# A linear-attention kernel with a token-wise maxout stage: attention stages dealt over slots, features dealt 3p+s, weights loaded second

## Chip, core and metric

The kernel runs on one core of a Trainium2 chip. What counts is the device time of one execution in microseconds. The core's engines run side by side, each through its own list of instructions in order, and wait for each other only where data or buffers ask for it: TensorE (PE, matmuls; PEld is its loading of weights), VectorE (DVE), ScalarE (ACT), GpSimd (POOL) and SyncE (SP, which issues the transfers).

## What is computed

Gated linear attention over 4 x 8 heads with 768 tokens and head size 48, then a maxout stage on the 3072 tokens with the 8 x 48 = 384 features of all heads:

```python
for t in range(S):
    state = alpha[:, :, t, :, None] * state + np.einsum('bhd,bhe->bhde', k[:, :, t], v[:, :, t])
    y[:, :, t] = np.einsum('bhd,bhde->bhe', q[:, :, t], state)
x = y.transpose(0, 2, 1, 3).reshape(B * S, H * D)
h1 = x @ w1
h2 = x @ w2
out = np.maximum(h1, h2) @ w_out
```

All inputs and the output are fp32; w1 and w2 are 384 x 1024, w_out is 1024 x 384.

## The kernel before

The recurrence is cut into chunks of 128 tokens, six for each of four batches, so 24 chunks `n`; a chunk covers all eight heads, taken as four pairs. The stages of a chunk are small functions:

- `load` (L62): four transfers (alpha, q, k, v) of 128 x 8 x 48 floats, issued by SP. Six buffers each.
- `a1` (ACT): `loga`, the logarithm of alpha. `p1` (PE): `cs`, its running sums by a triangular matrix, and four tiny matmuls for the decay of each half. `a2` (ACT): `en`, `ep`, `gg`, exponentials of it.
- `v1`: `qt` (DVE) and `kt` (POOL) are q and k times those; POOL also casts v into `v16`. `vt` (POOL) decays the running state `w` of the chunk before into `T16` and `t32`.
- `p2` (PE): eight transposes into `tp`; `v2` (DVE): `qk`, a copy of it. `p3` (PE): scores `pa`, `pb` and, in a batch's first five chunks, the state's increment `kv`. `v3` (DVE): two masked products `pt` and the new state `w`.
- `p4` (PE): y of the chunk, twelve matmuls of 96 output rows in four column groups, a head pair each (eight in a batch's first chunk). `a3` (ACT): copies it to `xT[0:96]`. So `xT` holds four head pairs of 96 features as four slabs. The maxout stage contracts 384 features as three slabs of 128: every third chunk, three transfers on ACT's queue (L265) move the fourth pair into rows 96 to 127 of the other three.

The maxout stage works on windows of 384 tokens, as max(h1, h2) = relu(h1 - h2) + h2. `fstep` (8 per window): three matmuls into a bank `h`, emptied through a relu into `g16` by DVE (three of eight) or ACT. `tstep` (one per 128 tokens): three matmuls with `m16` = w2 w_out and eight with `g16` and `wo16` into `op`; ACT copies it to `outs`, SP stores it. `prep_cast`, `prep_t` and `prep_m` make `wd16` = w1 - w2, `wo16` and `m16` once.

The order is written out by hand. A slot `n` is: `p2(n)`, `v2(n)`, `a2(n+1)`, gap 0, `a1(n+2)`, `p3(n)`, `v1(n+1)`, `v3(n)`, `vt(n+1)`, gap 1, `p1(n+2)`, `p4(n)`, `a3(n)`, gap 2. The gaps hold steps of the maxout stage by a fixed table: the eight `fstep`s of a window lie in the gaps of the slots after its last chunk, its `tstep`s in gap 2 of three slots after that. The last windows run after the last chunk. SP's list begins with chunks 0 to 2 and then the weights; chunk n+3 is issued in slot n. Matmul results lie in PSUM banks: `psx` (three: `cs`, `tp`, `kv`), `psp` (two: `pa`, `pb`) and `psm` (three: `y`, `h`, `op`).

Of the kernel before, what the change touches and what calls it, by code (L numbers as in the profile page):

```python
# [16 lines left out]
def kernel(  # L17
# [18 lines left out]
    nc = tc.nc  # L36
# [8 lines left out]
    W = 384  # L45
    CPW = W // C
    NW = NT // W
# [9 lines left out]

    nc.scalar.preload_act_table_set("natural_log_exp_and_others")
# [14 lines left out]
    for n in range(3):  # L73
        load(n)
# [49 lines left out]
    def a1(n):  # L124
        if n >= NCG:
            return
        af = loads[n][0]
        nc.scalar.activation(out=logas[n % NB][:, :, 0:D], in_=af, func=ACTF.Ln)  # L128

    def p1(n):  # L130
        if n >= NCG:
            return
        loga = logas[n % NB]
# [8 lines left out]
    def a2(n):  # L142
# [6 lines left out]
        gg = wk.tile([128, NP, 2], FP32, tag="gg", bufs=3)  # L149
# [19 lines left out]
    def vt(n):  # L169
        if n >= NCG:  # L170
            return
        s = st[n]
        if n % NCH:
            g = wk.tile([128, NP], FP32, tag="g")
            nc.gpsimd.tensor_mul(out=g[0:112], in0=st[n - 1]["gg"][0:112, :, 1], in1=s["gg"][0:112, :, 0])
            gb = g[0:112].unsqueeze(2).to_broadcast([112, NP, D])
            w = st[n - 1]["w"]
            T16 = T16s[n % 2]
            nc.gpsimd.tensor_mul(out=T16[0:48, :, 0:D], in0=w[0:48], in1=gb[0:48])  # L179
            nc.gpsimd.tensor_mul(out=T16[64:112, :, D : 2 * D], in0=w[64:112], in1=gb[64:112])  # L180
# [15 lines left out]
    def v2(n):  # L196
        qk = wk.tile([128, 2 * NP, 128], FP16, tag="qk")
# [201 lines left out]
```

## Time and profile before

| | us |
|---|---|
| median of 3 runs | 212.19 (212.09 to 214.8) |
| the profiled execution's own time | 212.77 |
| its span, first to last instruction | 211.0 |

| engine | busy us of the span | instructions |
|---|---|---|
| TensorE, matmul | 154.2 | 1440 |
| VectorE | 92.6 | 153 |
| ScalarE | 76.6 | 188 |
| GpSimd | 89.6 | 168 |

Busy time of TensorE counts each matmul from its start to its modelled end; matmuls overlap, so what they take in a row is read from their starts. The views that follow below are the windows (busy time of PE, PEld, DVE, ACT and POOL, in this order, in a stretch, with the granted clock of TensorE as a share of 2.4 GHz and what DMA moved), the waits (who waited for whom), the chain of waits (the work that ended last, followed back), the timeline and the groups of instructions by line. A chunk's slot is the unit in which to read them. L12 is line 12 of the kernel.

### The profile page before, as it was taken

To read this page: it belongs to the slowest core of one execution; us is meant where nothing else is said; L and a number is where in the kernel's file an instruction comes from. 1 tells how busy PE (TensorE), PEld (TensorE's weight loads), DVE (VectorE), ACT (ScalarE), POOL (GpSimd) and SP (SyncE) were. 2 spreads that over 40 slices of the span, in tenths; PEclk is the share of its full clock that TensorE was granted. 3 is DMA by queue.
4 is the path that set the end of the run, shared out by engine and by line. 5 is a ranking of instruction groups with operands and counts; after the bars stand their busy time and mean duration, and the time that the engine had idled before them with its cause. 6 is when DMAs were issued, how large, how long until landed. Compare 5 with 4: busy or idle time off the path is not lost.

```text
span 211.0 us, 3834 instructions
## 1 busy us (share of the span) xinstructions
PE 154.2 (73%) x1440; PEld 103.8 (49%) x1440; DVE 92.6 (44%) x153; ACT 76.6 (36%) x188; POOL 89.6 (42%) x168
## 2 busy tenths in 40 slices
PE   1182003757997599878888897988598988889993
PEld 1161002546665466455555564556365655555651
DVE  4255000776436557255655457344515755431200
ACT  3421000312553454434545425442424544315411
POOL 7267505654523575355335555342326545300000
PEclk9999999999999979999999999799859999999999
DMA  7999999999999006589777898389549741012122
GB/s 131 190 201 223 233 284 237 166 201 172 202 174 150 15 0 127 116 148 188 150 143 141 161 176 171 70 151 185 118 82 185 148 96 40 7 36 84 48 91 89
DMA packets 106339, 29.16 MB, mean 138 GB/s; under 512 B 100688, under 2 KB 105552, under 8 KB 106320
## 3 DMA queue, kind: packets, MB, share of 16 engines
q1 hardware_dynamic: 105168, 28.32, 70.6%
q10 hardware_dynamic: 1152, 0.59, 1.2%
q8 instruction: 11, 0.18, 0.4%
q14 instruction: 8, 0.07, 0.1%
HBM read 23.59 MB, written 4.72 MB: 134 GB/s over the span
## 4 chain that ended last, share of the span: by engine, by line
PE 37%; DVE 18%; SPq 15%; issue 10%; ACT 8%; ACTq 6%; DMA 4%; DVEq 0%
SPq L67 14%; PE op L313 12%; DVE pt L230 12%; PE y L251 7%; ACTq L265 6%; PE h L300 5%; PE op L311 5%; DVE qt L162 3%; DVE qk L198 3%; ACT xT L261 2%; PE mp L288 2%; DMA af<-in_alpha_dram 2%; PE y L247 2%; DMA xT<-xT 2%; ACT outs L316 2%
## 5 line engine op out<-in xcount | busy, mean ns | idle before, releaser
L163 POOL TENSOR_TENSOR kt<-kf,en 128x384 f16<-128x384 f32 x24 | 23.9, 996 | 56.6 <-ACT en L150 49.1
L300 PE MATMUL h<-xT,wd 128*128 128x384 f16 x192 | 42.0, 334 | 0.3 <-ACT outs L316 0.3
L198 DVE COPY qk<-tp 128x1024 f16<-128x1024 f16 x24 | 16.5, 689 | 56.1 <-PE tp L193 56.1
L313 PE MATMUL op<-wo,g 128*128 128x384 f16 x192 | 37.4, 341 | 0.0
L251 PE MATMUL y<-pt,v 128*96 128x128 f16 x192 | 24.8, 240 | 12.7 <-DVE pt L230 12.3
L261 ACT CAST xT<-y 96x512 f16<-96x512 f32 x24 | 14.0, 582 | 49.9 <-PE y L251 49.9
L135 PE MATMUL cs<-loga,cmat 128*128 128x384 f16 x24 | 8.9, 370 | 30.5 <-ACT loga L128 26.0
L162 DVE TENSOR_TENSOR qt<-qf,ep 128x384 f16<-128x384 f32 x24 | 23.1, 962 | 14.5 <-ACT ep L151 13.8
L303 DVE TENSOR_SCALAR g<-h 128x384 f16<-128x384 f32 x24 | 13.2, 550 | 30.8 <-PE h L300 30.8
L313 PEld LDWEIGHTS <-g 128*128 128x128 f16 x192 | 19.6, 102 | 14.1 <-issue 2.7
L316 ACT COPY outs<-op 128x384 f32<-128x384 f32 x24 | 11.5, 479 | 40.3 <-PE op L313 23.4
L139 PEld LDWEIGHTS <-loga 128*112 128x112 f16 x96 | 10.2, 152 | 31.8 <-issue 29.7
L251 PEld LDWEIGHTS <-v 128*96 128x96 f16 x192 | 20.1, 140 | 8.7 <-issue 8.4
L305 ACT ACTIVATE g<-h 128x384 f16<-128x384 f32 x40 | 19.9, 500 | 8.6 <-PE h L300 6.1
L128 ACT ACTIVATE loga<-af 128x384 f16<-128x384 f32 x24 | 12.9, 537 | 26.9 <-DMA af<-in_alpha_dram 25.0
L300 PEld LDWEIGHTS <-wd 128*128 128x128 f16 x192 | 16.7, 100 | 8.7 <-issue 0.9
L179 POOL TENSOR_TENSOR T<-w,g 48x192 f16<-48x192 f32 x20 | 10.0, 499 | 22.5 <-DVE w L238 16.6
L166 POOL CAST v<-vf 128x192 f16<-128x192 f32 x24 | 18.3, 761 | 0.0
L247 PE MATMUL y<-qk,T 112*96 112x128 f16 x80 | 17.4, 238 | 0.0
L230 DVE TENSOR_TENSOR pt<-pa,u 128x512 f16<-128x512 f32 x24 | 16.3, 680 | 2.2 <-PE pb L207 2.1
L207 PE MATMUL pa<-qk 48*128 48x128 f16 x96 | 10.5, 236 | 8.6 <-DVE qk L198 8.6
L311 PE MATMUL op<-m,xT 128*128 128x384 f16 x72 | 16.6, 342 | 0.0
(51 smaller groups left out, 211.2 us busy)
## 6 DMA issues: line engine op xcount, KB each, us to landing
af<-in_alpha_dram SPq DMA_DIRECT2D x24, 192.0 KB, 3.5
qf<-in_q_dram SPq DMA_DIRECT2D x24, 192.0 KB, 3.9
kf<-in_k_dram SPq DMA_DIRECT2D x24, 192.0 KB, 4.2
vf<-in_v_dram SPq DMA_DIRECT2D x24, 192.0 KB, 4.4
out_dram<-outs SPq DMA_DIRECT2D x24, 192.0 KB, 2.0
wof<-in_moe_w_out_dram SPq DMA_DIRECT2D x1, 1536.0 KB, 19.1
w2f<-in_moe_w_dram SPq DMA_DIRECT2D x1, 1152.0 KB, 9.2
w1f<-in_moe_w_dram SPq DMA_DIRECT2D x1, 1152.0 KB, 14.6
```

What stands on the lines that cost most here:

```text
L67: nc.sync.dma_start(out=t, in_=src[b, :, c * C : (c + 1) * C, :].rearrange("h p d -> p h d"))
L162: nc.vector.tensor_mul(out=qts[n % 2][:, :, 0:D], in0=qf, in1=s["ep"])
L163: nc.gpsimd.tensor_mul(out=kts[n % 2][:, :, 0:D], in0=kf, in1=s["en"])
L166: nc.gpsimd.tensor_copy(out=v16[:, :, 0:D], in_=vfp[:, :, 0, :])
L198: nc.vector.tensor_copy(out=qk, in_=st[n]["tp"])
L230: nc.vector.tensor_mul(out=pt[:, t], in0=s["pp"][t], in1=ub)
L247: nc.tensor.matmul(y[0:96, r, :], lhsT=T16s[n % 2][0:112, r, :], rhs=s["qk"][0:112, r, :], start=True, stop=False)
L251: nc.tensor.matmul(y[0:96, r, :], lhsT=v16[:, r, 48 * t : 48 * t + 96], rhs=s["pt"][:, t, r, :], start=(n % NCH == 0 and t == 0), stop=(t ...
L300: nc.tensor.matmul(h, lhsT=wd16[:, s, f * 128 : (f + 1) * 128], rhs=xT[:, s, w * W : (w + 1) * W], start=(s == 0), stop=(s == 2))
L305: nc.scalar.activation(out=gts[w][:, f, :], in_=h, func=ACTF.Relu)
L311: nc.tensor.matmul(op, lhsT=xT[:, s, t0 : t0 + 128], rhs=m16[:, s, :], start=(s == 0), stop=False)
L313: nc.tensor.matmul(op, lhsT=gts[w][:, f, i * 128 : (i + 1) * 128], rhs=wo16[:, f, :], start=False, stop=(f == NF - 1))
```

## The change

- The order of the stages. Slot `n` is now: `v1(n+1)`, `p4(n-1)`, `a3(n-1)`, gap, `a1(n+2)`, `p3(n)`, `v3(n)`, `vt(n+1)`, gap, `p2(n+1)`, `v2(n+1)`, gap, `p1(n+2)`, `a2(n+2)`. Chunk 0 and the preparation of the weights stand ahead of the slots. `qk` and `T16` get three buffers, `gg` four, `loga` two.
- What fills a gap. No table: a list `todo` of steps with a cost each; a gap takes steps up to a credit of 1.05 us. A `tstep` is cut in two. The steps of a group are put on the list once its last chunk's y is out. Groups are 1, 1, 1, 3, 3, 3, 3, 3, 3, 2, 1 chunks.
- Where y goes. Slab s of `xT` holds features 3p+s in row p. With v cast into that order (`v16` of three slabs of 16), head pair r of slab i is 32 rows, and its matmuls write `y[32r:32r+32, i]`: 36 matmuls of 32 output rows (24 in a batch's first chunk). The transfers of L265 go. w1 and w2 are read in the same order, a partition's three rows in one piece.
- Loads. Chunk 0, then the weights, then chunks 1 to 4; from then on a chunk is issued four slots ahead.
- Preparation. Casts and w1 - w2 are split over ACT, DVE and POOL.
- ACT empties six of the eight banks `h` of a window, DVE two.

```diff
-    for n in range(3):
+    load(0)
+    nc.sync.dma_start(out=w2f, in_=moe_w2.rearrange("(p s) f -> p s f", s=3))
+    nc.sync.dma_start(out=w1f, in_=moe_w1.rearrange("(p s) f -> p s f", s=3))
+    nc.sync.dma_start(out=wof, in_=moe_w_out.rearrange("(s p) d -> p s d", p=128))
+    for n in range(1, LD):
         load(n)
...
-        vfp = vf.rearrange("p (r t) d -> p r t d", t=2)
-        nc.gpsimd.tensor_copy(out=v16[:, :, 0:D], in_=vfp[:, :, 0, :])
-        nc.gpsimd.tensor_copy(out=v16[:, :, 96 : 96 + D], in_=vfp[:, :, 1, :])
+        vp = vf.rearrange("p (r t) (e s) -> p t r s e", t=2, s=3)
+        for t in range(2):
+            nc.gpsimd.tensor_copy(out=v16[:, :, :, 32 * t : 32 * t + 16], in_=vp[:, t])
...
     def p4(n):
...
-        y = psm.tile([128, NP, 128], FP32, tag="m", name="y")
+        y = psm.tile([128, 3, 128], FP32, tag="m", name="y")
...
+        for i in range(3):
+            if not first:
+                for r in range(NP):
+                    nc.tensor.matmul(
+                        y[32 * r : 32 * r + 32, i, :], lhsT=T16[0:112, r, i, :], rhs=s["qk"][0:112, r, :],
+                        start=True, stop=False,
+                    )
             for t in range(2):
-                nc.tensor.matmul(
-                    y[0:96, r, :],
-                    lhsT=v16[:, r, 48 * t : 48 * t + 96],
-                    rhs=s["pt"][:, t, r, :],
-                    start=(n % NCH == 0 and t == 0),
-                    stop=(t == 1),
-                )
+                for r in range(NP):
+                    nc.tensor.matmul(
+                        y[32 * r : 32 * r + 32, i, :], lhsT=v16[:, r, i, 16 * t : 16 * t + 32],
+                        rhs=s["pt"][:, t, r, :], start=(first and t == 0), stop=(t == 1),
+                    )
...
-        nc.scalar.copy(out=xT[0:96, :, n * C : (n + 1) * C], in_=st[n]["y"][0:96])
-        if n % CPW == CPW - 1:
-            w = n // CPW
-            for i in range(3):
-                nc.scalar.dma_start(
-                    out=xT[96:128, i, w * W : (w + 1) * W], in_=xT[32 * i : 32 * i + 32, 3, w * W : (w + 1) * W]
-                )
+        nc.scalar.copy(out=xT[:, :, n * C : (n + 1) * C], in_=st[n]["y"])
...
-        if f in (2, 4, 7):
+        if f in (3, 7):
...
+    for cpw in (1, 1, 1, 3, 3, 3, 3, 3, 3, 2, 1):
+        ends[a + cpw - 1] = (a * C, cpw)
+        a += cpw
+
+    def ready(n):
+        if n in ends:
+            a0, cpw = ends[n]
+            for f in range(NF):
+                todo.append((0.17 * cpw, fstep, (a0, cpw * C, f)))
+            for i in range(cpw):
+                todo.append((0.98, tstep, (a0, i, 0)))
+                todo.append((0.81, tstep, (a0, i, 1)))
...
+    def gap(us):
+        credit[0] = min(credit[0] + us, us)
+        while todo and credit[0] > 0:
+            cost, fn, args = todo.pop(0)
             fn(*args)
+            credit[0] -= cost
...
+    for n in range(1, NCG + 1):
+        if n - 1 + LD < NCG:
+            load(n - 1 + LD)
+        v1(n + 1)
+        if n > 1:
+            p4(n - 1)
+            a3(n - 1)
+        gap(1.05)
+        if n > 1:
+            ready(n - 1)
         if n < NCG:
...
             a1(n + 2)
             p3(n)
             v3(n)
+        vt(n + 1)
+        gap(1.05)
+        p2(n + 1)
+        v2(n + 1)
+        gap(1.05)
+        p1(n + 2)
+        a2(n + 2)
+    while todo:
+        gap(9.0)
```

VectorE's list in a slot in the middle of a batch, before: `qk` is the copy of slot n, `qt` belongs to chunk n+1, `pt` and `w` to chunk n, `g` is a feature step's relu.

```order
L198 COPY qk<-tp 128x1024
L162 TENSOR_TENSOR qt_125<-qf,ep 128x8x48
L230 TENSOR_TENSOR pt<-pa,u_108 128x512
L230 TENSOR_TENSOR pt<-pb,u_108 128x512
L238 TENSOR_TENSOR w<-kv,t_1003 112x192
```

The same engine in a slot of the changed kernel: `qt` is chunk n+1's, `pt` and `w` are chunk n's, `qk` is chunk n+1's.

```order
L157 TENSOR_TENSOR qt_152<-qf,ep 128x8x48
L231 TENSOR_TENSOR pt<-pa,u_135 128x512
L231 TENSOR_TENSOR pt<-pb,u_135 128x512
L239 TENSOR_TENSOR w<-kv,t_1208 112x192
L199 COPY qk<-tp 128x1024
```

The rows are the same five; `qk` has moved behind `pt` and `w` and belongs to the next chunk.

SP's list at the start, before, from chunk 2's loads on (af, qf, kf, vf are alpha, q, k, v):

```order
L67 DMA af<-in_alpha_dram 128x8x48
L67 DMA qf<-in_q_dram 128x8x48
L67 DMA kf<-in_k_dram 128x8x48
L67 DMA vf<-in_v_dram 128x8x48
L115 DMA w2f<-in_moe_w_dram 96x3x1024
L116 DMA w2f<-in_moe_w_dram 32x3x1024
L115 DMA w1f<-in_moe_w_dram 96x3x1024
L116 DMA w1f<-in_moe_w_dram 32x3x1024
L117 DMA wof<-in_moe_w_out_dram 128x8x384
```

And in the changed kernel, from the first row on:

```order
L66 DMA af<-in_alpha_dram 128x8x48
L66 DMA qf<-in_q_dram 128x8x48
L66 DMA kf<-in_k_dram 128x8x48
L66 DMA vf<-in_v_dram 128x8x48
L83 DMA w2f<-in_moe_w_dram 128x3072
L84 DMA w1f<-in_moe_w_dram 128x3072
L85 DMA wof<-in_moe_w_out_dram 128x8x384
L66 DMA af<-in_alpha_dram 128x8x48
```

The weights stand behind one chunk instead of three, in three transfers over all 128 partitions instead of five; the last row is chunk 1's alpha.

## Rows read from the trace of the kernel before

**Rows 1.** windows; columns: stretch, length, each engine's busy us (instructions), clock, DMA share, GB/s
```profile
0.00:6.00 6.00, 0.76 (x5) 0.70 (x6) 2.13 (x8) 1.81 (x2) 4.05 (x18) 1.00 0.77 139
20.00:34.00 14.00, 0.00 (x0) 0.00 (x0) 0.00 (x0) 0.00 (x0) 3.83 (x4) 1.00 1.07 260
80.00:110.00 30.00, 25.27 (x271) 16.76 (x269) 16.20 (x27) 14.24 (x37) 13.65 (x25) 1.00 0.75 148
```

**Rows 2.** waits of the span: engine, line, what ended them; us in total, times, longest
```profile
ACT loga L128 <- DMA af<-in_alpha_dram: 25.0, 4, 18.1
...
PE y L251 <- DVE pt L230: 12.3, 32, 2.2
PE pa L207 <- DVE qk L198: 8.6, 22, 0.8
```

**Rows 3.** chain of waits, in order of time: start us, us, what
```profile
58.03 1.30 PE mp L288 x8
...
82.27 1.18 DVE pt L230 x2
...
185.29 1.29 DVE pt L230 x2
...
206.19 1.31 PE op L313 x8
```

**Rows 4.** timeline of TensorE, one slot: start us, us, line, operation, tiles, count
```profile
113.31 0.39 PE L191 MATMUL tp<-ident,qt 128*128 128x128 f16 x4
113.53 0.39 PE L193 MATMUL tp<-ident,kt 128*128 128x128 f16 x4
...
114.70 0.23 PE L207 MATMUL pa<-qk 48*128 48x128 f16 x1 [0.30 <-DVE qk L198]
...
115.03 0.31 PE L216 MATMUL kv<-v,kt 128*64 128x48 f16 x8
115.27 0.66 PE L300 MATMUL h<-xT,wd 128*128 128x384 f16 x3
115.77 0.33 PE L135 MATMUL cs<-loga,cmat 128*128 128x384 f16 x1
...
116.11 0.24 PE L247 MATMUL y<-qk,T 112*96 112x128 f16 x1
...
117.12 0.22 PE L251 MATMUL y<-pt,v 128*96 128x128 f16 x1 [0.38 <-DVE pt L230]
...
117.69 0.65 PE L311 MATMUL op<-m,xT 128*128 128x384 f16 x3
118.18 1.46 PE L313 MATMUL op<-wo,g 128*128 128x384 f16 x8
119.48 0.65 PE L300 MATMUL h<-xT,wd 128*128 128x384 f16 x3
```

**Rows 5.** windows, 132 to 134 us, columns as in rows 1
```profile
132.00:134.00 2.00, 2.00 (x8) 0.99 (x7) 0.00 (x0) 0.12 (x1) 0.51 (x1) 0.50 0.38 56
```

**Rows 6.** groups of instructions by line: busy us, mean ns | idle before, releaser
```profile
L162 DVE TENSOR_TENSOR qt<-qf,ep 128x384 f16<-128x384 f32 x24 | 23.1, 962 | 14.5 <-ACT ep L151 13.8
...
L128 ACT ACTIVATE loga<-af 128x384 f16<-128x384 f32 x24 | 12.9, 537 | 26.9 <-DMA af<-in_alpha_dram 25.0 <-DVE qk L198 1.9
L151 ACT ACTIVATE ep<-cs 128x384 f32<-128x384 f32 x24 | 11.9, 496 | 0.0
L150 ACT ACTIVATE en<-cs 128x384 f32<-128x384 f32 x24 | 11.8, 493 | 1.9 <-issue 1.9
```

**Rows 7.** tile kv, 100 to 130 us: duration ns min/median/max
```profile
L216 PE MATMUL kv<-v,kt x32: 189/189/210, 108.5 to 128.0; 128*64 128x48 f16 x32
```

**Rows 8.** windows of one us in the loading stretch, columns as in rows 1
```profile
26.00:27.00 1.00, 0.00 (x0) 0.00 (x0) 0.00 (x0) 0.00 (x0) 0.00 (x0) 1.00 1.12 238
30.00:31.00 1.00, 0.00 (x0) 0.00 (x0) 0.00 (x0) 0.00 (x0) 0.00 (x0) 1.00 1.07 373
36.00:37.00 1.00, 1.00 (x11) 1.00 (x11) 0.00 (x0) 0.00 (x0) 0.48 (x1) 1.00 1.46 187
```

More of the change, by code (lines that the diff above doesn't have):

```diff
@@ L132, in p1 @@
             return
-        loga = logas[n % NB]
+        loga = logas[n % 2]
         cs = psx.tile([128, H * D + 2 * NP], FP32, tag="x", name="cs")
@@ L242, in p4 @@
         s = st[n]
[L243 removed]
+        y = psm.tile([128, 3, 128], FP32, tag="m", name="y")
         v16 = v16s[n % NB]
[L245 to L257 removed]
+        T16 = T16s[n % NB]
@@ L277, in prep_t, with prep_wd, prep_wo @@
+    def prep_wd():
+        for s in range(2):
+            nc.vector.tensor_sub(out=wd16[:, s, :], in0=w1f[:, s, :], in1=w2f[:, s, :])
+        nc.gpsimd.tensor_sub(out=wd16[:, 2, :], in0=w1f[:, 2, :], in1=w2f[:, 2, :])
+    def prep_wo():
+        nc.gpsimd.tensor_copy(out=wo16[:, 0:3, :], in_=wof[:, 0:3, :])
+        nc.scalar.copy(out=wo16[:, 3:6, :], in_=wof[:, 3:6, :])
+        nc.vector.tensor_copy(out=wo16[:, 6:8, :], in_=wof[:, 6:8, :])
     def prep_t(f):
@@ L320 @@
-    LAG = 1
-    gaps = {}
-    def put(slot, gap, fn, *args):
-        gaps.setdefault((slot, gap), []).append((fn, args))
-    for w in range(NW):
-        s0 = CPW * (w + 1) + LAG
-        for f in range(NF):
-            put(s0 + f // 3, f % 3, fstep, w, f)
-        for i in range(3):
-            put(s0 + 3 + i, 2, tstep, w, i)
-    put(2, 0, prep_cast)
-    for f in range(0, NF, 2):
-        put(2 + f // 4, 1 + (f // 2) % 2, prep_t, f)
-    for s in range(3):
-        put(4, s, prep_m, s)
@@ L338, in gap, with tstep @@
-    def gap(slot, i):
-        for fn, args in gaps.get((slot, i), ()):
+        if f in (3, 7):
+            nc.vector.tensor_relu(gts[a][:, f, 0:W], h[:, 0:W])
+        else:
+            nc.scalar.activation(out=gts[a][:, f, 0:W], in_=h[:, 0:W], func=ACTF.Relu)
+    ops = {}
+    def tstep(a, i, half):
+        t0 = a + i * C
+        if half == 0:
+            op = ops[t0] = psm.tile([128, DM], FP32, tag="m", name="op")
+            for s in range(3):
+                nc.tensor.matmul(op, lhsT=xT[:, s, t0 : t0 + C], rhs=m16[:, s, :], start=(s == 0), stop=False)
+        op = ops[t0]
+        for f in (range(3) if half == 0 else range(3, NF)):
+            nc.tensor.matmul(op, lhsT=gts[a][:, f, i * C : (i + 1) * C], rhs=wo16[:, f, :],
+                             start=False, stop=(f == NF - 1))
+        if half:
+            os_ = mo.tile([128, DM], FP32, tag="outs", name="outs", bufs=3)
+            nc.scalar.copy(out=os_, in_=op)
+            nc.sync.dma_start(out=out[t0 : t0 + C, :], in_=os_)
@@ L340, in gap @@
             fn(*args)
+            credit[0] -= cost
     a1(0)
     p1(0)
-    a1(1)
     a2(0)
     v1(0)
-    p1(1)
-    last = max(s for s, _ in gaps)
-    for n in range(max(NCG, last + 1)):
-        if n < NCG:
-            if n + 3 < NCG:
-                load(n + 3)
-            p2(n)
-            v2(n)
-            a2(n + 1)
-            gap(n, 0)
+    p2(0)
+    v2(0)
+    p3(0)
+    v3(0)
+    prep_w2()
+    prep_t(0)
+    prep_t(2)
+    p4(0)
+    a3(0)
+    prep_t(4)
+    prep_t(6)
@@ L357 @@
+    prep_wd()
+    prep_wo()
+    a1(1)
+    p1(1)
+    a2(1)
+    ready(0)
+    v1(1)
+    gap(1.3)
+    vt(1)
+    p2(1)
+    v2(1)
+    for s in range(3):
+        prep_m(s)
+    a1(2)
+    p1(2)
+    a2(2)
+    for n in range(1, NCG + 1):
[8 more added lines that the diff above has]
+            ready(n - 1)
+        if n < NCG:
             a1(n + 2)
             p3(n)
-            v1(n + 1)
@@ L360 @@
             v3(n)
-            vt(n + 1)
-            gap(n, 1)
-            p1(n + 2)
-            p4(n)
-            a3(n)
-            gap(n, 2)
-        else:
-            for i in range(3):
-                gap(n, i)
+        vt(n + 1)
[7 more added lines that the diff above has]
+        gap(9.0)
 _INS = ['q', 'k', 'v', 'alpha', 'moe_w1', 'moe_w2', 'moe_w_out']
```

123 lines of the change are left out of this document (54 added, 69 removed).

## The prediction

> **What bounds the kernel now.** I read the windows first, then the chain of waits, then one slot of the matmul timeline. The span falls into three parts. In the first, TensorE does nothing from 20 to 34 us while DMA runs at 260 GB/s [rows 1]: the weights are queued behind three chunks, chunk 3's alpha lies behind the weights, and ScalarE waits 25.0 us in four waits for alpha [rows 2]. In the second, one chunk a slot goes through. On the chain the pair of `pt` products stands at 82.27 us for chunk 8 and at 185.29 us for chunk 23 [rows 3]: 15 slots in 103.0 us, 6.87 us a slot. In the third, from 185.29 us to 211.0, hardly anything is left but matmuls of the token windows; the last ends at 206.19 + 1.31 = 207.5 [rows 3].
>
> In the slots no engine is full: from 80 to 110 us (4.37 slots) VectorE is busy 16.20 us, ScalarE 14.24, GpSimd 13.65 [rows 1], so 3.7, 3.3 and 3.1 us a slot. What TensorE needs is read from the starts of its matmuls, since their durations overlap [rows 4]. Transposes (`p2`): four in 0.22 us, so 0.44. Scores and `kv` (`p3`): 114.70 to 115.27, 0.57. `p1`: 115.77 to 116.11, 0.34. `p4`: ten matmuls from 117.12 to 117.69, 57 ns each, 0.68 for twelve. Feature steps: three matmuls in 0.50, eight steps per three chunks, 1.33 a slot. A token step: 0.49 + 1.30 = 1.79. Sum 5.15 us. So 1.7 us of 6.87 are waits and slow-clock stretches: `p3` waits for `qk` (8.6 us in 22 waits) and `p4` for `pt` (12.3 in 32) [rows 2], and at each such place nothing else is queued on TensorE that it could do in the meantime. One stretch runs at a granted 0.50, the 1.2 GHz level [rows 5].
>
> **The change, part by part.**
>
> *Stages a slot apart.* Now `p4(n-1)`, about 1.05 us of token work, `p3(n)`, token work, `p2(n+1)`, token work, `p1(n+2)` follow each other on TensorE. `pt(n-1)` was made in the slot before; `qk(n)` was copied at the end of the slot before, with `p1`, `p4` and 1.05 us of token work between `p2(n)` and `p3(n)`. `qt(n+1)` has `p4`, a gap, `p3` and a gap (3.4 us) between `ep` and `p2`, and needs 0.96 [rows 6]. So both waits lose their cause. What is late next: feature steps take a bank of the three of `psm` each, and ScalarE empties it in order, behind `en`, `ep` and `xT`. For this I put 0.28 us a slot (bounds: nothing, and the 1.7 us of now; nearer the lower one, as ScalarE is free for half a slot).
>
> *y straight into place.* Twelve matmuls of 96 output rows become 36 of 32, in four column quarters (24 in the first chunk of each batch). No row shows quarters. Bounds: if all four quarters overlap fully, 9 x 57 = 0.51 us; if nothing overlaps and each costs what one of the twelve costs, 36 x 57 = 2.05. The nearest row is `kv`, which goes in column halves: one takes 189 ns [rows 7], eight end 0.31 us after the first starts [rows 4], so (310 - 189)/7 = 17 ns from one to the next. They fill 0.24 us with entry and exit [rows 4], 0.12 more than seven steps of 17. I take 36 x 17 + 120 = 0.73, say 0.75. The price beside before's 0.68 is next to nothing. What it buys: the three transfers per window that moved the fourth head pair into place on the ScalarE queue go, and `xT` is 384 columns instead of 512.
>
> The Trainium skill speaks against this part: TensorEngine Tiling (Array Packing), section Instruction Overhead, says that a matmul carries about 60 cycles however few its columns. At 2.4 GHz that is an estimate of 25 ns each, 0.90 us for 36, and 3 us more on the whole time than by the 17 ns that the trace shows.
>
> *Slot after.* 5.15 - 0.68 + 0.75 + 0.28 = 5.50 us. Other engines: ScalarE takes six of eight feature evictions instead of five, a sixth of a slot more at most; VectorE one less; GpSimd reads v with a stride, and even at 1.5 times all its time it stays at 4.7. DMA: a chunk's four loads are 0.786 MB, at 187 GB/s [rows 8] 4.2 us; the 0.197 MB of output cost 0.5 us at 373 GB/s and 1.05 at 187. So 4.7 to 5.25, under 5.5, though not by much.
>
> *Weights second.* Chunk 0 is in at about 6 us (139 GB/s x 6 is 0.83 MB, [rows 1]). Then come 4.72 MB of weights: 12.7 us at 373 GB/s or 19.8 at 238 [rows 8], since before saw both rates in the weights' transfers; in the middle they are in at 22. Preparing `w2` (transposes) is hidden under the other two weights. Chunk 1's alpha is in at 23.1, the chunk at 26.2, and each later one 4.2 us after. From alpha: `loga` 0.54, `p1` 0.34, `en` and `ep` 0.99, `qt` 0.96 [rows 6], to 25.9; `p2(1)` stands behind the eight small feature steps and their evictions, to about 28. Behind it `prep_m`, three times 1.30 [rows 3], to 32. Chunk 2 repeats the 2.8 us from `loga` to `qt`, then `p2`, `p1(3)` and handovers: slot 2 starts at about 37. From there chunk n+2 is always in before it is needed: chunk 4 at 38.8, slot 3 at 42.5.
>
> *End.* Slots 2 to 23 are 22 x 5.50 = 121, less `p1` in slot 22 and `p1`, `p2` in slot 23 (1.1): slot 24 starts at 156.9. It has `p4(23)`, 0.75. Token work left over by then, counted in the program's own credits, which agree with the rows (3.15 a chunk beside 1.33 + 1.79): the group of chunks 18 to 20 has had 8 gaps of 1.05 for its 9.45, 1.05 is left; the group of two 6.3; the last of one 3.15; together 10.5. Then 3.5 us from the last matmul to the end, as now (207.5 to 211.0). 156.9 + 0.75 + 10.5 + 3.5 = 171.7 us of span. The profiled run was 212.77 with a span of 211.0, so 1.8 lie around it: 173.5 us. Its own time is 0.6 above the median of 212.19, which I leave in.
>
> **Rivals.**
> 1. *The 36 matmuls don't overlap:* `p4` costs 2.05, 1.30 more in 23 slots: 173.5 + 30 = 203. For it: no row shows quarters or so many small matmuls in a row, and the eight of `kv` could have been queued while TensorE waited. Against it: 17 ns in the halves. Here TensorE: Matmul & The Clock Gate of the Trainium skill (section "Wait - 56ns, not 53.3ns?") gives 62 ns a matmul where the sequencer decodes them in software; by that it would be 2.2 us in place of 2.05. The trace contradicts it for eight in a row, not for 36. Chance 0.09.
> 2. *A new wait holds the slot at 6.0 us:* banks of `psm`, or loads plus output if they reach only 165 GB/s together. 22 x 0.5 = 11: 184.5. For it: DMA's floor lies close under the slot, and a wait in order is easily met. Chance 0.18.
> 3. *The clock:* if 20 us of work run at 0.50 as in [rows 5], they cost 10 more: 183.5. That stretch came after waits of `p4`, which go. Chance 0.07.
> 4. *Slower:* each change of column quarter costs what entering and leaving the halves costs (0.12), 36 x 137 ns = 4.9 us: 4.2 more in 23 slots, 270 us. It decides from 2.4 us a `p4`, 67 ns a matmul, more than an unpacked one takes now (57). Against it: `kv` changes halves with every matmul at 17 ns. Chance 0.04.
>
> **Numbers.** The forecast has 0.62, with a range of its own of 163 (slot 5.15, weights at 373 GB/s) to 182 (slot 5.8, weights at 238). With rivals 2 and 3 that is 0.87; at the edges of these a few hundredths fall outside, so 163 to 190 holds 8 in 10. About 2% is what a measurement of this kernel tells from no change. Faster by more than that are the forecast and rivals 1 to 3 nearly whole, 0.94; within it 0.02; slower 0.04.
>
> **What would show it.** In the profile after: TensorE has work from 26 us on; `p4`'s 36 matmuls start about 17 ns apart and the stage fills 0.75 us (at 57 ns rival 1, above 67 rival 4); slots are 5.3 to 5.7 us apart; the waits of `p3` for `qk` and of `p4` for `pt` are near nothing; some 11 us of token work stand behind the last `p4`. The forecast is wrong if the 36 crawl, if TensorE waits more than 0.5 us a slot for `psm`, for `loga` or for loads, or if slot 2 starts after 42 us.

## The result, and the profile of the changed kernel

| | before | after |
|---|---|---|
| median | 212.19 us | 163.22 us (162.66 to 165.21, 4 runs) |
| the profiled execution | 212.77, span 211.0 | 163.15, span 161.4 |

The ratio of after to before is 0.7665, with a 95% interval of 0.7601 to 0.7729: faster, as forecast, and by 10 us more than the 173.5 forecast. The lower edge of the range was 163.0: the median lies 0.2 us above it, the ratio times 212.19 (162.6) 0.4 below, so the time stands at that edge, which the prediction gave for a slot of 5.15 us and weights at 373 GB/s.

The first view is the same as in [rows 2], the waits of TensorE over the whole span (who waited for whom; us in total, times, longest):

```profile
PE cs L130 <- ACT loga L123: 10.0, 3, 4.6
...
PE pa L208 <- DVE qk L199: 1.4, 3, 0.8
...
PE h L308 <- ACT g L313: 0.6, 3, 0.2
```

Of the two waits that cost a slot its time before, `p4` for `pt` (12.3 us in 32 waits) isn't there at all, and `p3` for `qk` has gone from 8.6 us in 22 to 1.4 in 3. The 10.0 us for `loga` lie ahead of slot 2: one wait each for chunk 0, chunk 1 (4.62 us, at 21.41) and chunk 2 (0.99, at 30.74).

The second view is the y stage of one slot on TensorE (start us, us, line, operation, tiles, count), the counterpart of the `y` rows in [rows 4]:

```profile
95.01 0.24 PE L252 MATMUL y<-qk,T 112*32 112x128 f16 x4
95.08 0.29 PE L258 MATMUL y<-pt,v 128*32 128x128 f16 x8
95.19 0.23 PE L252 MATMUL y<-qk,T 112*32 112x128 f16 x4
95.25 0.28 PE L258 MATMUL y<-pt,v 128*32 128x128 f16 x8
95.36 0.23 PE L252 MATMUL y<-qk,T 112*32 112x128 f16 x4
95.42 0.29 PE L258 MATMUL y<-pt,v 128*32 128x128 f16 x8
95.64 0.66 PE L322 MATMUL op<-m,xT 128*128 128x384 f16 x3
```

The next step starts 0.63 us after the first of the 36 matmuls. Twelve of them take 0.175 us (95.01, 95.19, 95.36), so 14.6 ns each: the four quarters do overlap. 36 of these are 0.53 us, which is the prediction's lower bound of 0.51 (four quarters overlapping fully) but for 0.02.

The third view shows the slots by ScalarE's copies of y to `xT`, one a chunk (chunks 1, 3, 4, 5, 6, 12, 18 and 23 here):

```profile
35.42 0.49 ACT L265 CAST xT<-y 128x384 f16<-128x384 f32 x1
...
46.74 0.49 ACT L265 CAST xT<-y 128x384 f16<-128x384 f32 x1
49.81 0.49 ACT L265 CAST xT<-y 128x384 f16<-128x384 f32 x1
53.70 0.48 ACT L265 CAST xT<-y 128x384 f16<-128x384 f32 x1
59.58 0.49 ACT L265 CAST xT<-y 128x384 f16<-128x384 f32 x1
...
90.75 0.49 ACT L265 CAST xT<-y 128x384 f16<-128x384 f32 x1
...
121.90 0.49 ACT L265 CAST xT<-y 128x384 f16<-128x384 f32 x1
...
146.32 0.48 ACT L265 CAST xT<-y 128x384 f16<-128x384 f32 x1 [1.09 <-PE y L258]
```

From chunk 12 to 18 six slots take 31.15 us, 5.19 each (6.87 before, [rows 3]). Two slots near the start take only 3.07 and 3.89 us. They turn out to be the step where the prediction failed.

The chain of waits ends as before with a token step (start us, us, what):

```profile
156.17 1.31 PE op L325 x8
```

The last matmul ends at 157.48, the span at 161.4.

### The profile page after: what moved, and what is told of

It reads as the page before. It is cut to its first block, busy times and chain, and to the rows that moved or that the text cites. A ratio compares the mean times of both kernels' runs of the same rounds, so it can differ in the third digit from the quotient of the medians.

```text
span 161.4 us, 5077 instructions
## 1 busy us (share of the span) xinstructions
PE 139.1 (86%) x2056; PEld 95.2 (59%) x2056; DVE 92.9 (58%) x153; ACT 81.3 (50%) x216; POOL 91.5 (57%) x170
## 4 chain that ended last, share of the span: by engine, by line
PE 78%; DMA 9%; ACT 3%; SPq 2%; issue 2%; DVE 2%; POOL 1%; ACTq 0%; DVEq 0%; POOLq 0%
PE h L308 22%; PE op L325 20%; DMA wof<-in_moe_w_out_dram 9%; PE op L322 8%; PE y L258 5%; PE pa L208 4%; PE y L252 3%; PE tp L192 3%; PE tp L190 3%; PE kv L217 3%; PE mp L296 2%; PE cs L130 2%; PE cs L134 2%; SPq L66 2%; DVE pt L231 1%
## 5 line engine op out<-in xcount | busy, mean ns | idle before, releaser
L308 PE MATMUL h<-xT,wd 128*128 128x384 f16 (+2 forms) x264 | 40.2, 295 | 1.0 <-ACT g L313 0.6
L313 ACT ACTIVATE g<-h 128x384 f16<-128x384 f32 (+2 forms) x66 | 25.2, 410 | 10.7 <-PE h L308 10.4
L308 PEld LDWEIGHTS <-wd 128*128 128x128 f16 x264 | 22.0, 103 | 10.6 <-issue 2.6
L162 POOL CAST v<-vf 128x192 f16<-128x192 f32 x48 | 26.9, 587 | 0.0
L145 ACT ACTIVATE en<-cs 128x384 f32<-128x384 f32 x24 | 11.7, 489 | 15.7 <-PE cs L134 14.0
L231 DVE TENSOR_TENSOR pt<-pb,u 128x512 f16<-128x512 f32 x24 | 16.3, 678 | 0.0
L258 PE MATMUL y<-pt,v 128*32 128x128 f16 x576 | 15.7, 226 | 0.0
L311 DVE TENSOR_SCALAR g<-h 128x384 f16<-128x384 f32 (+2 forms) x22 | 9.7, 440 | 10.3 <-PE h L308 10.3
L265 ACT CAST xT<-y 128x384 f16<-128x384 f32 x24 | 11.8, 490 | 3.9 <-PE y L258 3.9
L258 PEld LDWEIGHTS <-v 128*32 128x32 f16 x576 | 11.8, 100 | 0.5 <-issue 0.4
```

The lines of the kernel that those rows point to most:

```text
L162: nc.gpsimd.tensor_copy(out=v16[:, :, :, 32 * t : 32 * t + 16], in_=vp[:, t])
L231: nc.vector.tensor_mul(out=pt[:, t], in0=s["pp"][t], in1=ub)
L258: nc.tensor.matmul(y[32 * r : 32 * r + 32, i, :], lhsT=v16[:, r, i, 16 * t : 16 * t + 32], rhs=s["pt"][:, t, r, :], start=(first and t == ...
L308: nc.tensor.matmul(h[:, 0:W], lhsT=wd16[:, s, f * 128 : (f + 1) * 128], rhs=xT[:, s, a : a + W], start=(s == 0), stop=(s == 2))
L313: nc.scalar.activation(out=gts[a][:, f, 0:W], in_=h[:, 0:W], func=ACTF.Relu)
```

## The experiments

All runs are compared with the kernel before on the same chip. The changed kernel's own time is taken as 163.0 us, between its two medians (163.22, and 162.77 for the control below). The runs were on several chips, on which the median of the kernel before lies between 210.16 and 212.19, so a difference of about 1 us between two runs on different chips tells nothing.

| run | what it does | median us | ratio to before (95%) |
|---|---|---|---|
| quarter_by_quarter | the 36 matmuls in another order | 179.93 | 0.851 (0.845 to 0.857) |
| old_y | y as before, with the transfers | 210.99 | 0.999 (0.996 to 1.003) |
| old_y_lag | the same, read a slot later | 179.10 | 0.851 (0.846 to 0.855) |
| unskewed | stages in the old order | 174.85 | 0.828 (0.822 to 0.834) |
| two_banks | one bank less for `y`, `h`, `op` | 172.92 | 0.817 (0.812 to 0.823) |
| weights_fourth | weights behind three chunks | 171.32 | 0.814 (0.807 to 0.821) |
| before_weights_second | kernel before, weights second | 219.19 | 1.032 (1.021 to 1.042) |
| groups_of_three | eight groups of three chunks | 166.86 | 0.788 (0.781 to 0.794) |
| early_ones | six groups of one at the start | 166.50 | 0.788 (0.782 to 0.794) |
| early_alpha | a step moved ahead of slot 2 | 163.78 | 0.778 (0.773 to 0.783) |
| thin_start | less token work a gap in slots 2 to 5 | 161.21 | 0.766 (0.761 to 0.771) |
| after_again | the changed kernel again | 162.77 | 0.769 (0.764 to 0.775) |

### Is it the four quarters that make 36 matmuls cheap?

In *quarter_by_quarter* the same 36 matmuls are issued with all nine of one quarter in a row instead of going around the quarters.

```diff
-        for i in range(3):
-            if not first:
-                for r in range(NP):
+        for r in range(NP):
+            for i in range(3):
+                if not first:
...
-            for t in range(2):
-                for r in range(NP):
+                for t in range(2):
```

> The changed kernel, with the 36 matmuls of y issued quarter after quarter (nine in a row into the same column quarter) instead of round the four quarters; same matmuls, same output. Theory A (the stage is cheap because four quarters run side by side): each costs at least the 57 ns of one of before's twelve, so the stage goes from 0.63 us to about 2.05 us, 1.4 us more in 23 slots, 163.2 + 33 = 196 us. Rival B (a small matmul is cheap by itself, about 15 ns to issue, whatever quarter it goes to): no change, 162 to 165 us.

The y stage of one slot, TensorE's timeline:

```profile
90.67 0.23 PE L252 MATMUL y<-qk,T 112*32 112x128 f16 x1
90.74 0.28 PE L257 MATMUL y<-pt,v 128*32 128x128 f16 x2
90.85 0.22 PE L252 MATMUL y<-qk,T 112*32 112x128 f16 x1
...
92.20 0.99 PE L324 MATMUL op<-wo,g 128*128 128x384 f16 x5
```

The stage takes 1.53 us instead of 0.63: 42 ns a matmul instead of 17.5, with what frames the stage in both. Three matmuls of one quarter and slab take 0.18 (90.67 to 90.85), some 60 ns each, like the unpacked ones [rows 4]; the mean is lower because those at a change of quarter overlap. The step into the next slab is in these 0.18 us, and it goes to another place in PSUM, so it is the quarter that the matmuls share which holds them apart, and not the place that they add into. So it is the turn around the quarters that makes the stage cheap. A slot takes 5.93 us on average (chunks 5 to 20) against 5.23 in the changed kernel, and the kernel 17 us more. The forecast's upper bound, 36 x 57 = 2.05 us with nothing overlapping, wasn't reached even so, and neither was theory A's 196 us; rival B, no change, is out.

### What do the transfers into the fourth slab cost?

*old_y* has y as before: twelve matmuls of 96 rows, four slabs, and three transfers on ACT's queue per group. This layout also wants w1 and w2 in four transfers, as before.

```diff
-        nc.scalar.copy(out=xT[:, :, n * C : (n + 1) * C], in_=st[n]["y"])
+        nc.scalar.copy(out=xT[0:96, :, n * C : (n + 1) * C], in_=st[n]["y"][0:96])
+        if n in ends:
+            a0, cpw = ends[n]
+            for i in range(3):
+                nc.scalar.dma_start(
+                    out=xT[96:128, i, a0 : a0 + cpw * C], in_=xT[32 * i : 32 * i + 32, 3, a0 : a0 + cpw * C]
+                )
```

> The changed kernel with y, v and the weights laid out as before: twelve matmuls of 96 rows, xT in four slabs, three transfers on ScalarE's queue at the end of each group, five weight transfers; everything else as changed. Theory A (the direct place is worth the transfers' wait): from the copy of y to the landing of the third transfer it takes about 4 us, of which the gap and p3 cover 1.6, so about 2.4 us in each of the groups that have nothing left to do, and some stall of ScalarE: 163.2 + 15 to 24 = 178 to 187 us. Rival B (hidden): up to 168 us.

It gave the whole gain back: 210.99 us, 24 more than the upper end of theory A. TensorE's timeline from the last `kv` of a group's last chunk on:

```profile
89.62 0.31 PE L216 MATMUL kv<-v,kt 128*64 128x48 f16 x8
92.76 0.34 PE L312 MATMUL h<-xT,wd 128*128 128x384 f16 x1 [2.84 <-DMA xT<-xT]
93.86 0.48 PE L312 MATMUL h<-xT,wd 128*128 128x384 f16 x1 [0.76 <-DMA xT<-xT]
94.55 2.40 PE L312 MATMUL h<-xT,wd 128*128 128x384 f16 x7 [0.21 <-DMA xT<-xT]
```

And the windows behind it (stretch, length, busy us of PE, PEld, DVE, ACT, POOL, clock, DMA share, GB/s):

```profile
90.00:92.00 2.00, 0.00 (x0) 0.00 (x0) 1.35 (x3) 0.81 (x2) 1.05 (x4) 1.00 1.20 206
92.00:94.00 2.00, 0.48 (x2) 0.21 (x3) 0.00 (x0) 0.09 (x1) 1.01 (x2) 0.95 1.12 214
94.00:96.00 2.00, 1.79 (x6) 0.69 (x5) 0.00 (x0) 0.49 (x1) 0.00 (x0) 0.50 0.64 143
```

ScalarE begins to issue the transfers at 89.35, behind the copy, and the feature steps that the list puts right behind the y stage wait until 94.55 for the last of them. From issue to landing a transfer takes 3.2 us (median) and up to 5.6; in the kernel before it was 2.2. Then the clock stands at 0.50, the 1.2 GHz level. Over the span TensorE waits 27.0 us for `xT` in 17 waits, and its mean granted clock is 0.919 instead of 0.989. Once per group of three a slot takes 10 to 13 us in place of 5.4; the others take 4.7 to 5.4 as in the changed kernel. The loss is that fresh y is wanted at once and comes through DMA engines that the loads keep busy (DMA share 1.1 to 1.2).

*old_y_lag* is old_y with the steps of a group put on the list a slot later:

```diff
-        if n > 1:
-            ready(n - 1)
+        if n > 2:
+            ready(n - 2)
...
+    ready(NCG - 1)
```

> The changed kernel with y, v and the weights laid out as before and the transfers back (as in old_y), but a group's token work is put on the list one slot later, so that the transfers have a slot to land, as they had in the kernel before. Theory A (what old_y lost is the wait of the first feature step for the transfers, 4 to 5 us a group since they land behind the loads, and the half clock that follows such a wait): with a slot of lag the wait is covered; what stays is the transfers' issue on ScalarE's queue, the last group's landing (4 us) and one slot more of token work at the end: 168 to 176 us. Rival B (the transfers themselves hurt, by ScalarE's queue or by the DMA engines, wherever the token work stands): over 185 us.

179.10 us, 3 over theory A's range, and a single wait of 0.2 us for `xT` is left; slots take 5.32 on average (chunks 5 to 20), against 5.23 in the changed kernel. So two thirds of old_y's loss (32 of 48 us) were the wait and the low clock behind it. Of the other third, 6.7 us are the start: chunk 1's copy stands at 42.16 us instead of 35.42. The rest is 2.9 us in the slots up to chunk 6, 3.8 in those up to chunk 23, and 2.1 behind the last copy, where the lag itself leaves more to do. The windows of the loading stretch, first of old_y_lag, then of the changed kernel:

```profile
8.00:12.00 4.00, 1.07 (x18) 0.64 (x16) 2.25 (x4) 0.00 (x0) 0.03 (x1) 1.00 1.03 244
12.00:16.00 4.00, 0.00 (x0) 0.00 (x0) 0.69 (x1) 1.02 (x1) 0.98 (x1) 1.00 1.02 236
```

```profile
8.00:12.00 4.00, 1.13 (x18) 0.64 (x16) 2.51 (x5) 0.27 (x1) 0.51 (x2) 1.00 0.98 406
12.00:16.00 4.00, 3.01 (x43) 2.35 (x44) 1.55 (x3) 1.26 (x2) 1.80 (x2) 1.00 0.99 387
```

The same bytes of w1 and w2 come in at 236 to 244 GB/s in four transfers over 96 and 32 partitions, and at 387 to 406 in two transfers over all 128 with a partition's three rows in one piece. Which of the two differences does it, the number of partitions or the length of a piece, was not tried apart. The kernel before speaks for the partitions: w_out, over all 128 in pieces of one row (1.5 KB, shorter than a row of w1), came in at 373 GB/s there, after w1 and w2 had landed (30 to 31 us in [rows 8]).

### What is the order of the stages worth?

*unskewed* keeps everything else and puts the stages of a chunk into one slot, in the order that the kernel before had.

```diff
+        p2(n)
+        v2(n)
+        a2(n + 1)
+        gap(1.05)
+        a1(n + 2)
+        p3(n)
         v1(n + 1)
-        if n > 1:
-            p4(n - 1)
-            a3(n - 1)
...
+        v3(n)
         vt(n + 1)
         gap(1.05)
-        p2(n + 1)
-        v2(n + 1)
+        p1(n + 2)
+        p4(n)
+        a3(n)
+        ready(n)
         gap(1.05)
-        p1(n + 2)
-        a2(n + 2)
```

> The changed kernel with the stages of a slot in the order of before (p2, p3, p4 of one chunk in one slot, the same three gaps between them); y's new place, the loads, the groups and the credit stay. Theory A (the order takes away the waits of p3 for qk and of p4 for pt, about 1.0 to 1.4 us a slot): a slot goes from 5.2 to 6.2 to 6.6 us, 185 to 193 us. Rival B (what counted in the slots was the three transfers a window on ScalarE's queue and the token work spread evenly; the order itself is worth little): under 170 us.

174.85 us, 11.8 over the changed kernel: between the two theories, less than was expected of the order and more than nothing. TensorE's timeline at one y stage and behind it:

```profile
110.04 0.24 PE L258 MATMUL y<-pt,v 128*32 128x128 f16 x4 [0.19 <-DVE pt L231]
...
111.20 1.62 PE L308 MATMUL h<-xT,wd 128*128 128x384 f16 x9 [0.58 <-ACT xT L265]
```

The wait of `p4` for `pt` is back (3.0 us in 9 over the span, 12.3 in 32 before), and feature steps now wait for the fresh `xT` (4.6 us in 8); `p3` waits for `qk` no more often than in the changed kernel (3 times). The waits are small because the gaps of the list stand between the stages; a slot is 5.67 us (chunks 12 to 18) against 5.19. Of the 1.68 us by which a slot got shorter, the order as such is 0.5.

*two_banks* asks whether the allowance of 0.28 us a slot for banks of `psm` was a real cost: the pool has two instead of three.

```diff
-    psm = ctx.enter_context(tc.tile_pool(name="psm", bufs=3, space=bass.MemoryType.PSUM))
+    psm = ctx.enter_context(tc.tile_pool(name="psm", bufs=2, space=bass.MemoryType.PSUM))
```

> The pool that y, h and op share has two banks instead of three. Theory A (banks come free well before they are asked for, so the allowance of 0.28 us a slot for such waits should have been nothing): 162 to 166 us. Theory B (the third bank is only just enough, and the allowance was close to a true cost): TensorE waits at h for ScalarE's relu in every slot, 0.3 us a slot or more, 169 to 180 us.

172.92 us against 162.77 of the control beside it. Six slots (copies of chunks 12 and 18) take 32.6 us, 5.44 each. TensorE's timeline has waits such as this one, which the changed kernel has not:

```profile
96.18 0.65 PE L308 MATMUL h<-xT,wd 128*128 128x384 f16 x3 [0.39 <-ACT xT L265]
```

So the time is theory B's: with two banks a slot costs 0.25 us more, and with three such waits are nothing: from 90 to 121 us TensorE's waits list is empty in the changed kernel. But they don't come in every slot, nor behind the relu, as theory B had it: from 60 to 150 us the list has six, 1.8 us, all behind the copy of y, which is less than half of what the slots lose there. And the slots up to chunk 23 are only 4 of the 10 us; 2.0 us are there before chunk 1's copy, 1.4 come up to chunk 6 and 2.1 behind the last copy. The allowance had the right size for a kernel with one bank less.

### What is the place of the weights worth?

```diff
-    load(0)
+    for n in range(3):
+        load(n)
...
-    for n in range(1, LD):
+    for n in range(3, LD):
```

> The changed kernel with three chunks ahead of the weights in SP's list, as before. Theory A (TensorE's list has the preparation of the weights ahead of chunk 1, so all waits for the weights, which land two chunks of 4.2 us later): slot 2 starts at 43 us instead of 34.4, 163.2 + 8.4 = 171.6 us. Rival B (the two chunks loaded early are needed anyway, and slots 4 to 6, which have little to do, take the shift up): 163 to 166 us.

*weights_fourth* gave 171.32, 8.3 us over the changed kernel. ScalarE's timeline (start us, us, what, idle before and what ended it):

```profile
20.20 1.04 ACT L272 CAST w<-w2f 128x1024 f16<-128x1024 f32 x1 [14.12 <-DMA w2f<-in_moe_w_dram]
...
29.26 0.52 ACT L124 ACTIVATE loga<-af 128x384 f16<-128x384 f32 x1
```

Chunk 1's `loga` starts at 29.26 instead of 20.84 in the changed kernel, since ScalarE's list has the weights' casts ahead of it. From there on all copies are 8 to 10 us later with the same distances: the start moves the end one for one.

Is the place of the weights a gain by itself? *before_weights_second* is the kernel before with only that:

```diff
-    for n in range(3):
-        load(n)
+    load(0)
...
     load_weights()
+    for n in range(1, 3):
+        load(n)
```

> The kernel before with only its list of loads changed: chunk 0, the weights, chunks 1 and 2. Theory A (the place of the weights pays only with the list of token steps that can start early and with loads five chunks ahead; in the old order the same bytes lie ahead of chunk 3's alpha, which ends ScalarE's wait at 34.7 us, and the steps of the first group stand in slot 4 by a fixed table): 208 to 213 us. Theory B (bringing the weights in early is a gain by itself, some 8 us as the run with the weights fourth suggests): 200 to 205 us.

Neither theory held: 219.19 us, 3.2% slower than before. VectorE's timeline shows where (`wd` is w1 - w2), first the kernel before, then this run:

```profile
38.93 3.80 DVE L274 TENSOR_TENSOR wd<-w1f,w2f 128x3072 f16<-128x3072 f32 x1
```

```profile
40.42 9.11 DVE L274 TENSOR_TENSOR wd<-w1f,w2f 128x3072 f16<-128x3072 f32 x1
```

GpSimd's timeline of this run beside it:

```profile
39.64 2.74 POOL L273 CAST w<-w2f 128x3072 f16<-128x3072 f32 x1
42.33 2.75 POOL L275 CAST wo<-wof 128x3072 f16<-128x3072 f32 x1
45.04 0.99 POOL L163 TENSOR_TENSOR kt<-kf,en 128x384 f16<-128x384 f32 x1
...
46.26 3.48 POOL L167 CAST v<-vf 128x192 f16<-128x192 f32 x1
```

Before, GpSimd's two large casts were done early, at 22.7 and 33.7, as the weights came in, and the subtraction took 3.80 us; a cast of v that started 0.5 us after it took 3.47. Here all the preparation is released at once, in slot 2, and the subtraction takes 9.11; TensorE's y stage then waits 6.74 us for `pt`, which stands behind it on VectorE. The last 3.8 us of the 9.11 begin at 45.7, about where GpSimd's row of operations ends, and the small cast that starts at 46.26 takes 3.48 us instead of 0.34 and ends with the subtraction. So one engine seems to wait while the other goes through, rather than both going slowly. The Trainium skill says so: SBUF — State Buffer, section "Who interferes with whom", has VectorE and GpSimd take an exclusive lock on a shared pair of ports, and these times agree with it. Who goes first is not simply who came first: the subtraction started at 40.42 and yet waited for GpSimd's operations that began at 42.33 and 45.04. From chunk 3 on the slots are about those of the kernel before, 5 to 7 us late.

In the changed kernel the preparation is split into thirds over three engines ahead of the slots, and its two parts of the subtraction on VectorE take 1.43 us each. So the weights' place is worth 8.3 us beside the other changes, and by itself it loses 3%; how the 8.3 are shared out between the split, the shape of the transfers and the list of steps was not tried.

### Groups and the start

*groups_of_three* has eight groups of three instead of 1, 1, 1, 3, 3, 3, 3, 3, 3, 2, 1:

```diff
-    for cpw in (1, 1, 1, 3, 3, 3, 3, 3, 3, 2, 1):
+    for cpw in (3, 3, 3, 3, 3, 3, 3, 3):
```

> The changed kernel with eight token groups of three chunks instead of 1, 1, 1, 3, 3, 3, 3, 3, 3, 2, 1. Theory A (small first and last groups give TensorE work early and leave less at the end): slots 1 to 3 have nothing to fill them, a short slot there saves little because each waits on its own chain, and 6.3 us more token work stands behind the last chunk: 163.2 + 4 to 6 = 167 to 169 us. Rival B (the token work is the same and only moves): 162 to 165 us.

166.86: the small groups are worth 3.9 us, though not for the reason that theory A gives. Behind the last copy it takes 14.0 us, not more than the changed kernel's 15.1; all of the loss is at the start, where chunk 6's copy stands at 64.50 instead of 59.58. From 38 to 46 us the granted clock is 0.50 there, so how much of the 3.9 us is the groups' and how much the clock's is open. *early_ones* has chunks 3, 4 and 5 in groups of one as well; it is the test of the prediction's failed step.

```diff
-    for cpw in (1, 1, 1, 3, 3, 3, 3, 3, 3, 2, 1):
+    for cpw in (1, 1, 1, 1, 1, 1, 3, 3, 3, 3, 3, 2, 1):
```

> The groups of chunks 3, 4 and 5 are one chunk each instead of one group of three. Theory A (slots 4 and 5 of the changed kernel are short, 3.1 and 3.8 us, only because no group is ready then; token work that isn't done early is done late, and none of it is done twice): slots 4 and 5 grow to about 5.2 us, and the short slots move to 7 and 8, where now nothing is ready; the time stays at 162 to 166 us. Theory B (those slots are short for another reason, such as prepared chunks standing in line): slots 4 and 5 stay under 4.2 us, slots 7 and 8 stay at 5.2, and the time falls by what is then missing at the end, to under 160 us.

ScalarE's copies of chunks 3 to 9:

```profile
47.47 0.49 ACT L265 CAST xT<-y 128x384 f16<-128x384 f32 x1
53.37 0.49 ACT L265 CAST xT<-y 128x384 f16<-128x384 f32 x1
59.17 0.49 ACT L265 CAST xT<-y 128x384 f16<-128x384 f32 x1
65.08 0.49 ACT L265 CAST xT<-y 128x384 f16<-128x384 f32 x1
68.15 0.49 ACT L265 CAST xT<-y 128x384 f16<-128x384 f32 x1
72.61 0.48 ACT L265 CAST xT<-y 128x384 f16<-128x384 f32 x1
78.35 0.49 ACT L265 CAST xT<-y 128x384 f16<-128x384 f32 x1
```

The slots that were 3.07 and 3.89 us are 5.90 and 5.80 now, and two short ones of 3.07 and 4.46 stand three slots later, where now no group is ready. That is theory A. The time, 166.50, is half a microsecond over theory A's span and 3.7 over the control on the same chip: a slot with a group of one takes 5.8 to 5.9 instead of 5.2, in part since its short feature steps (0.17 us for three matmuls) wait for ScalarE's relu (1.0 us in 5 waits from 41 to 65 us), and the start was 0.7 later.

*early_alpha* moves a third of the preparation of `m16` behind chunk 2's first stages, to bring slot 2 forward:

```diff
-    for s in range(3):
-        prep_m(s)
+    prep_m(0)
+    prep_m(1)
     a1(2)
...
+    prep_m(2)
```

> The changed kernel with loga, cs and the exponentials of chunk 2 put between the second and the third part of prep_m instead of behind all three. Theory A (slot 2's start hangs on chunk 2's alpha, whose logarithm stands behind the last copy of prep_m on ScalarE at 30.2 us while the alpha is there by 29): slot 2 starts 1.0 to 1.5 us earlier, 161.7 to 162.3 us. Rival B (the token step of chunk 0 or DMA holds slot 2 anyway): 163 us.

163.78, no gain: chunk 1's y stage starts at 34.88 us, and 34.44 in the changed kernel. What was moved is TensorE's work, and the token step that stands there needs it in any case: at 31.86 TensorE waits 0.24 us for its result.

*thin_start* gives the gaps of slots 2 to 5 a credit of 0.55 instead of 1.05, so that the token work on hand stretches over the slots that have none:

```diff
+    GAP = [0.55 if 1 < n < 6 else 1.05 for n in range(NCG + 1)]
...
-        gap(1.05)
+        gap(GAP[n])
```

> The changed kernel with a credit of 0.55 us a gap instead of 1.05 in slots 2 to 5, so that the token work of chunks 1 and 2 is spread over these slots and slots 4 and 5 are not left without any. Theory A (in 34 to 53 us of the changed kernel TensorE waits about 3 us and then runs 4 us at half clock; both go): 158.5 to 161.5 us, and no granted clock under 0.9 after 40 us. Rival B (these slots are held by the loads, or the work is only moved): 163 us, half clock or not.

161.21 us, the fastest of all runs. Windows of the changed kernel around the empty slots:

```profile
50.00:52.00 2.00, 0.84 (x13) 0.50 (x14) 1.75 (x3) 0.73 (x2) 1.86 (x4) 1.00 1.10 217
52.00:54.00 2.00, 2.00 (x53) 1.68 (x53) 1.01 (x2) 1.23 (x4) 1.32 (x3) 0.69 0.60 103
54.00:56.00 2.00, 2.00 (x17) 1.03 (x14) 2.00 (x4) 0.96 (x3) 1.60 (x4) 0.50 1.03 238
```

The same of thin_start:

```profile
50.00:52.00 2.00, 2.00 (x27) 1.50 (x26) 2.00 (x4) 0.71 (x2) 1.37 (x3) 1.00 1.07 214
...
54.00:56.00 2.00, 2.00 (x20) 1.35 (x19) 1.98 (x5) 1.47 (x3) 1.24 (x4) 1.00 1.01 195
```

In the changed kernel TensorE is idle for 1.16 of the two us before 52, and its clock falls to the 1.2 GHz level behind it; in thin_start neither happens. But the idle time alone doesn't tell when the clock falls: weights_fourth has the same matmuls with the same waits 9.6 us later, and its clock stays at full speed:

```profile
60.00:62.00 2.00, 0.86 (x13) 0.65 (x12) 1.35 (x4) 0.32 (x1) 1.92 (x4) 1.00 1.14 223
62.00:64.00 2.00, 1.74 (x59) 1.42 (x58) 1.41 (x2) 1.64 (x5) 1.32 (x3) 1.00 0.48 86
```

So that thin_start keeps the clock up is seen, and that it does so by its fuller slots is likely but not shown. From chunk 1's copy to chunk 7's it takes 27.2 us instead of 29.4, and 28.2 in weights_fourth: 1.2 of the 2.2 us are the clock, the rest the slots themselves. Its ratio overlaps that of the changed kernel (0.766 against 0.767 and 0.769); on its own chip it stands 1.6% below early_alpha, which has the changed kernel's slots. So it is about 1% faster by the trace, and not shown to be by the ratios.

*after_again* is the control that ran beside early_ones and two_banks.

> The changed kernel once more, as a control for the runs beside it: 162 to 164.5 us, with the y stage of chunk 5 starting at 58 to 59 us and slots of 5.2 us from there on. Another number would mean that chips differ by more than the comparisons show.

162.77 us with the copy of chunk 6 at 59.5, and 59.58 before: the changed kernel repeats.

## Where the prediction held, and where it failed

**Held: the waits go.** `p3` and `p4` stopped waiting, no new wait took their place, and the slot came out at 5.19 instead of 5.50 us. Rival 2 (a slot of 6.0) didn't come: DMA kept up, and three banks suffice.

**Held: the quarters overlap.** 14.6 ns a matmul instead of the 17 taken from the halves, 0.63 us a stage instead of 0.75. Rivals 1 and 4 fall with it. The rule that spoke against this part, 60 cycles a matmul in the Trainium skill's TensorEngine Tiling (Array Packing), section Instruction Overhead, would by the prediction's estimate have made 0.90 us; the measured 0.63 decides against it here.

**Mis-sized: the wait allowance.** This is the largest part of the miss. A slot's 5.19 less its matmuls (5.15 - 0.68 + 0.63 = 5.10) leaves 0.09 for waits and handovers, not 0.28. With the y stage this is 0.31 a slot; over slots 7 to 23 the trace has 86.7 us (copies at 59.58 and 146.32), where 17 slots of 5.50 less 1.1 make 92.4: 5.7 us of the miss, of which 17 x 0.31 explains 5.3.

**Mis-sized: the weights' rate.** Slot 2 was forecast at 37.0, with 238 to 373 GB/s for the weights; they came at 376 to 406, over the upper bound, `wo` was in at 19.8 us instead of 22, and slot 2 began at 34.44 us: 2.6 us earlier. The lower bound came from transfers of w1 and w2 in another shape, over 96 and 32 partitions in pieces of one row, and old_y_lag has their 240 GB/s again; the upper one was w_out's rate, over all 128, and the new transfers of w1 and w2 go with that one.

**Failed: the token work was counted twice.** In the sum this is the step that was wrong in kind and not only in size: "22 x 5.50 ... Token work left over by then ... together 10.5". Each of the 22 slots was charged its full 3.12 us of token work (1.33 + 1.79), 68.6 in all, and then 10.5 more behind slot 24: 79.1. But there are 24 chunks, 75 us of it, and group 0's 3.1 is done before slot 2: 72 are left. 7 us stood in the sum that no engine had to do. In the trace they are missing where the list is empty: slots 4 and 5 take 3.07 and 3.89 instead of 11.0 together (4.0 us less), because the groups of one are used up and the group of chunks 3 to 5 isn't complete. By the list's credits slots 2 to 6 get 8.9 us of work instead of 15.6; chunk 1's copy to chunk 6's takes 24.2 us instead of 27.5, so about half of the 7 us came out as time, and the rest went into waits there (1.04 us for `kt` at 51.96) and the low clock. early_ones showed that the short slots go where the list is empty. The prediction had the list's groups and credits before it; it counted what was left at the end by credits and forgot to count what was missing at the start.

The account, from the forecast span of 171.7 to the measured 161.4, by the copies, which start a y stage later than the slots: chunk 1's at 35.42 instead of 37.0 + 0.75, -2.3; slots 2 and 3, 11.3 us instead of 11.0, +0.3; slots 4 and 5, -4.0; slot 6, 5.9 instead of 5.5 with the clock low, +0.4; slots 7 to 23, -5.7; from the last copy to the end 15.1 instead of 10.5 + 3.5, +1.1. Together -10.2, of the 10.3 by which the span was off.

**Rival 3, the clock.** It came, but small: 20 us of work at 0.50 were put at 10 us. There was one such stretch, 52.5 to 56 us. In thin_start and in weights_fourth, without it, the same slot takes 4.82 us instead of 5.88: 1.06 us.

**Held, without its cause: the gain as a whole.** The forecast gave the order 1.37 us a slot (6.87 to 5.50) and the y stage next to nothing. By the runs the order is 0.5 us a slot and 11.8 us in all. y straight into place is 16 us where the list waits a slot for the transfers (0.09 us a slot; 6.7 of the 16 are the start), and 48 where it doesn't. The prediction named the transfers as something that goes, and didn't price them. Order and place together don't make up the 1.68 us a slot. What is left, some 1.1 us, no run takes away by itself; the first candidate is the list that fills the gaps, which is in all of these runs and in place of which the fixed table was never put back. So where the larger part of the gain in the slots comes from stays open.

## What to carry to other kernels

When work is dealt into slots from a list, write a ledger: all the work there is, what is done before, what each slot can take from what is ready by then, and what is left; a sum of full slots plus a tail counts some of it twice. When a consumer moves closer to its producer, ask what lies between them: a transfer that was hidden by a slot of distance costs its whole way once the distance is gone. And undo one part at a time before believing which part of a change brings the gain: here the order was worth a third of what was forecast, and the early weights, a gain beside the rest, were a loss alone.

## What the runs showed of the hardware

- Matmuls of 32 output rows that go around the four column quarters start 14.6 ns apart (36 in 0.63 us with what frames them); with nine in a row in the same quarter, some 60 ns within it, and 36 take 1.53 us.
- Loads over 128 partitions with a partition's three rows in one piece ran at 376 to 406 GB/s from 8 to 18 us. The Trainium skill (DMA: Bandwidth & Descriptors, section "Where 436 GB/s comes from") puts the limit for HBM at about 358 and that of the fabric at 435; the measured rate lies between them, so the lower limit did not hold here.
- Transfers of 8 to 24 KB within SBUF took up to 5.6 us from issue to landing, 3.2 in the median, in old_y, where loads kept the DMA share at 1.1 to 1.2.
- A subtraction on VectorE took 9.11 us instead of 3.80 beside GpSimd's casts, and a cast on GpSimd 3.48 instead of 0.34 beside the subtraction: one waited while the other went through.
- TensorE's clock fell to the 1.2 GHz level right after two us with only 0.84 us of matmuls, and in old_y after nearly 3 us of waiting; in weights_fourth it stayed at full speed after two us with 0.86 us of the same matmuls.
